# Windowed attention and two feed-forward layers in one kernel: output sums behind a group's last products, three PSUM tiles in the last group, conversions moved beside h, and another start address for x's operands

## The chip, the cores and the metric

The kernel runs on one core of a Trainium2 chip. The metric is the device time in microseconds; lower is better. Its engines are named as in the profile: PE multiplies matrices (PEld loads its stationary operand), DVE, ACT and POOL work element by element, and SP issues most of the DMAs. PE accumulates in PSUM, from which DVE and ACT read.

## What is computed

Windowed attention over q, k, v (4 batches, 8 heads, 576 positions, window 64) gives x of 2304 x 512. Two feed-forward layers follow; the change is in the second and in the end of the first:

```python
a, b = x @ w1, x @ w2
x2 = (a * b @ w3) @ w_out          # first layer, 2304 x 512
h = x2 @ w_in                      # second layer, 2304 x 2048
g = h * (1 / (1 + np.exp(-h)))
out = g @ w_out2                   # 2304 x 512
```

## The kernel before

Every float32 product is made of three passes over a high and a low part of each operand (`PASSES`). The program is written out by hand in one order for each engine, and an engine runs its instructions in that order; a scheduler moves nothing.

The part around the change has four stages.

- **Phase a, block 5** (`phase_a(NBLK - 1, hooks5)`): the last block of 384 tokens of the first layer, 16 steps of 12 matmuls (L693) and 96 more (L723). Four PSUM accumulators take turns. ACT copies every other one out (L707), DVE multiplies the next by the copy (L709), ACT and POOL split the product. `hooks5` puts the first operands of stage h between these steps: loads of x2 and w_in32, sums of them, splits (`x_sum`, `x_op`, `w_part`).
- **Stage h**: h by Strassen's scheme with 7 products for each d of 12 (3 supers of 768 tokens by 4 duos of features); a product is 12 matmuls 384 wide. `h_slot` issues one product, then its read-out (`read`: DVE sums, ACT silu), then what the table `jobs` holds for that slot. Four sums of silu(h) per d go to DRAM (`keep`, tensor `gd`). A **conversion** (`convert`) turns two blocks of w_out2 from 64-bit words into float32 with sums, and stores them in DRAM (`t32`): ten slots of loads, ACT scalings (L220, L225), DVE bit operations (L228, L884), POOL adds. Conversions 0 and 1 stand in block 5, 2 to 7 in stage h, by the table `PLAN`.
- **The passage** from h to the output: the jobs of the last super load the converted weights (`o_load`), split them (`o_part`), and prepare the first output operands from `gd` (`f_load`, `f_sums`, `f_high`, `f_low`). Output products 0 to 3 are issued between the last products of h.
- **Output**: 36 output products (`out_products(m)`), each 42 matmuls 256 wide; four of them (e = 0 to 3) make a group, 128 rows on either side. Product m needs `hi` and `lo` of m, in one of four sets that take turns, so that `f_high(m + 3)` waits until product m - 1 has read its set. A group accumulates in two PSUM tiles, `a` and `b`, of two banks each; odd and even groups use different ones. `out_sums` makes the output of a group's seven terms: an ACT copy of A11, four DVE adds and a last one, each called as soon as its term's last matmuls (e = 3) are issued:

```python
                if e == DUOS - 1:
                    out_sums(tg, op)
```

The terms S2 and S3 share bank 1 of `a`, S1 and A22 share bank 0 of `a`, A12 and S4 bank 0 of `b`. A tile is guarded as a whole: a matmul that is issued after a sum of the same tile waits for that sum. In the pool `end` a tile of 96 bytes, `e0`, stands ahead of the tiles x0 to x6 that hold x's operands (`xop`), so each starts 96 bytes past a multiple of 128; the operands of phase a (xa, xb, p, q) start at multiples of 128.

Of the kernel before, what the change touches and what calls it, by code (L numbers as in the profile page):

```python
# [9 lines left out]
F32 = mybir.dt.float32  # L10
# [32 lines left out]
def tile_window_attention_ffn(ctx, tc, qkv, qkp, vp, w1, w2, w3t, w_out, w_in, w_out2, out):  # L43
# [7 lines left out]
    nc = tc.nc  # L51
# [3 lines left out]
    dram = ctx.enter_context(tc.tile_pool(name="dram", bufs=1, space=DRAM))  # L55
# [76 lines left out]
    class Chunk:  # L132
# [14 lines left out]
        begun = False  # L147
# [600 lines left out]
    with tc.manual_schedule():  # L748
# [5 lines left out]
        for i in range(16):  # L754
            qq, k = divmod(i, 4)
# [34 lines left out]
        OPS = 7  # L790
        POS = (0, 1, 6, 2, 4, 3, 5)
        HALF = slice(0, NB), slice(NB, 2 * NB)
        gd = dram.tile([NTG, DUOS, 128, 4, 256], F32, name="gd", tag="gd")
        t32 = dram.tile([PAIRS, 128, 7, 256], F32, name="t32", tag="t32")
        xop, raw, wop, oop = {}, {}, {}, {}
        g, bank, tmp = {}, {}, {}
# [5 lines left out]
        def add(eng, out, a, b):  # L802
            tt(eng, out, a, b, ALU.add)
# [220 lines left out]
        def silu(out, src):  # L1024
            nc.scalar.activation(out=out, in_=src, func=AF.Silu)

        def keep(d, op, t):
            j, e = divmod(d, DUOS)
            nc.sync.dma_start(
                out=gd[3 * j : 3 * j + 3, e, :, op, :].rearrange("t p n -> p t n"),  # L1030
                in_=t.rearrange("p t q n -> p t (q n)"),
            )

        def read(d, k):

# [94 lines left out]


        A11, A12, A22, S1, S3, S2, S4 = range(7)
        TERMS = ((A11, 0, 0), (S2, 2, 1), (S3, 0, 1), (S1, 2, 0), (A22, 3, 0), (A12, 1, 0), (S4, 1, 1))
        AT = (("b", 1, 0), ("a", 1, 0), ("a", 1, 1), ("a", 0, 1), ("a", 0, 0), ("b", 0, 0), ("b", 0, 1))
        FIRST = (True, True, False, True, False, True, False)

        def out_products(m):
            tg, e = divmod(m, DUOS)
            if e == 0:
                for x, y in (("a", "ha"), ("b", "hb")) if tg % 2 == 0 else (("a", "hc"), ("b", "hd")):  # L1140
                    bank[x] = pso.tile([128, 2, 512], F32, name=f"o{x}{tg}", tag=y)
            lo, hi, a = sets.pop(m)
            for (op, w, half), (x, y, z), first in zip(TERMS, AT, FIRST):
                dst = bank[x][:, y, z * 256 : z * 256 + 256]
                for q in range(2):
                    cols = slice(q * 128, q * 128 + 128)
                    lhs = [x[:, cols] for x in a] if op == S4 else [hi[:, op, cols], lo[:, op, cols]]
                    rhs = [x[:, half] for x in oop[2 * e + q][w]]
                    for n, (l, r) in enumerate(PASSES):
                        nc.tensor.matmul(  # L1150
                            dst, lhsT=lhs[l], rhs=rhs[r], start=(first and e == 0 and q == 0 and n == 0),
                            stop=(e == DUOS - 1 and q == 1 and n == 2), skip_group_check=True,
                        )
                if e == DUOS - 1:
                    out_sums(tg, op)

        def out_sums(tg, op):

            a, b = bank["a"], bank["b"]
# [6 lines left out]
            row = j * 2 * NB + r * 128  # L1169
            if op == A11:  # L1170
                nc.scalar.copy(out=one, in_=b[:, 1, 0:256])
            elif op == S2:
                add(nc.vector, two, a[:, 1, 0:256], one)
            elif op == S3:
                add(nc.vector, u3, a[:, 1, 256:512], two)
            elif op == S1:
                add(nc.vector, u4, a[:, 0, 256:512], two)
            elif op == A22:
                x = a[:, 0].rearrange("p (i n) -> p i n", i=2)
                add(nc.vector, c[:, 1], x, t[:, 3:4].to_broadcast([128, 2, 256]))  # L1180
                nc.sync.dma_start(out=out[row + NB : row + NB + 128, :], in_=c[:, 1].rearrange("p i n -> p (i n)"))
            elif tg == NTG - 1:
                i = 1 if op == S4 else 0
                add(nc.vector, c[:, 0, i], b[:, 0, i * 256 : i * 256 + 256], t[:, i])
                (nc.sync if i else nc.scalar).dma_start(
                    out=out[row : row + 128, i * 256 : i * 256 + 256], in_=c[:, 0, i]
                )
            elif op == S4:
                add(nc.vector, c[:, 0], b[:, 0].rearrange("p (i n) -> p i n", i=2), t[:, 0:2])
                nc.sync.dma_start(out=out[row : row + 128, :], in_=c[:, 0].rearrange("p i n -> p (i n)"))  # L1190


        X5 = {2: (x_sum, 0), 3: (x_op, 0, 0), 4: (x_sum, 2), 5: (x_sum, 1), 7: (x_op, 0, 1), 9: (x_op, 0, 2)}
# [3 lines left out]
        def hooks5(n):  # L1197
            run_later()
            if n == 0:
                tmp["t1"] = xe[:, 1536:2304].rearrange("p (k n) -> p k n", k=2)  # L1200
                x_raw(0)
                e0 = end.tile([128, 24], F32, name="e0", tag="e0")[:, 0:1]
                nc.gpsimd.memset(e0, 0.0)
                silu(e0, e0)
                places = [slot(f"wd{i}", f"x{i}", [1024], pool=end) for i in range(2, 6)]
                for i, (first, x) in enumerate(((2, 2), (6, 0))):
                    convert(i, n5 + first, places[x : x + 2])
                r_load(0, slot("r0", "x6", [1024], pool=end))
# [22 lines left out]
        for j in range(1, SUPER):  # L1231
# [10 lines left out]
        for n, first in ((0, 2), (1, 10), (2, 12), (3, 16), (4, 18), (5, 23), (6, 24)):  # L1242
            for part in range(4):
# [3 lines left out]
        at(FIRST_OUT + 22, f_load, 0)  # L1247
        at(FIRST_OUT + 22, f_load, 1)
        at(FIRST_OUT + 24, f_sums, 0, nc.vector)
        at(FIRST_OUT + 25, f_high, 0)  # L1250
        at(FIRST_OUT + 26, f_low, 0)
        at(FIRST_OUT + 26, f_sums, 1, nc.vector)
        at(FIRST_OUT + 27, f_load, 2)
        at(FIRST_OUT + 27, o_load, 7)

        phase_a(NBLK - 1, hooks5)
# [126 lines left out]
```

## Time and profile before

| | |
|---|---|
| median of 3 runs | 892.2 us (889.32 to 894.3) |
| profiled execution | 890.85 us |
| its span (first to last instruction) | 888.3 us, mean granted clock 0.976 |
| PE busy | 831.2 us (94%) |
| DVE / ACT / POOL busy | 656.5 / 542.5 / 388.1 us |

Times in rows are microseconds from the span's start. The profiled execution lies 2.5 us over its own span and 1.35 us under the median. A busy PE is the time in which some matmul is under way; how fast they follow each other has to be read from their starts.

### The profile page before, as it was taken

To read this page: it belongs to the slowest core of one execution; us is meant where nothing else is said; L and a number is where in the kernel's file an instruction comes from. 1 tells how busy PE (TensorE), PEld (TensorE's weight loads), DVE (VectorE), ACT (ScalarE), POOL (GpSimd) and SP (SyncE) were. 2 spreads that over 40 slices of the span, in tenths; PEclk is the share of its full clock that TensorE was granted. 3 is DMA by queue.
4 is the path that set the end of the run, shared out by engine and by line. 5 is a ranking of instruction groups with operands and counts; after the bars stand their busy time and mean duration, and the time that the engine had idled before them with its cause. 6 is when DMAs were issued, how large, how long until landed. Compare 5 with 4: busy or idle time off the path is not lost. (4 is left out here: it accounts for less than half of the span.)

```text
span 888.3 us, 15643 instructions
## 1 busy us (share of the span) xinstructions
PE 831.2 (94%) x5066; PEld 779.0 (88%) x5066; DVE 656.5 (74%) x1527; ACT 542.5 (61%) x1290; POOL 388.1 (44%) x468
## 2 busy tenths in 40 slices
PE   8899999999999999999879999999984988888887
PEld 3455899999999999999779999999984988888887
DVE  8879777788888888882885798665688667677561
ACT  7889778898898998984554555444553333333230
POOL 5767666677776776774651243400002111111100
PEclk9999999999999999999999999999987899899899
DMA  9997235345445455435234879968755233233210
GB/s 309 337 293 237 76 99 165 108 138 186 135 149 173 138 163 168 148 99 179 112 131 131 247 232 278 303 189 243 240 187 160 95 119 119 96 120 112 89 61 24
DMA packets 78256, 146.34 MB, mean 165 GB/s; under 512 B 7136, under 2 KB 46432, under 8 KB 78176
## 3 DMA queue, kind: packets, MB, share of 16 engines
q1 hardware_dynamic: 74576, 140.50, 49.0%
q10 hardware_dynamic: 3600, 4.85, 1.5%
q8 instruction: 40, 0.66, 0.3%
q14 instruction: 40, 0.33, 0.1%
HBM read 105.48 MB, written 39.85 MB: 164 GB/s over the span
## 5 line engine op out<-in xcount | busy, mean ns | idle before, releaser
L693 PE MATMUL ab<-xa,hl 128*128 128x384 f32 x576 | 119.7, 342 | 5.0 <-DVE a L709 3.4
L1150 PE MATMUL oa<-wo_w,hi 128*128 128x256 f32 x432 | 85.5, 293 | 32.4 <-DVE ot L800 32.4
L693 PE MATMUL ab<-xb,hl 128*128 128x384 f32 x570 | 115.2, 334 | 0.0
L693 PEld LDWEIGHTS ab<-xa,hl 128*128 128x128 f32 x576 | 98.7, 188 | 6.8 <-DVE a L709 4.5
L1150 PEld LDWEIGHTS oa<-wo_w,hi 128*128 128x128 f32 x432 | 67.8, 194 | 38.4 <-DVE ot L800 38.4
L693 PEld LDWEIGHTS ab<-xb,hl 128*128 128x128 f32 x570 | 100.3, 188 | 0.0
L800 POOL TENSOR_TENSOR fs<-f 128x256 f32<-128x256 f32 x11 | 10.2, 928 | 153.0 <-DMA f<-gd 141.0
L351 POOL TENSOR_TENSOR klo<-qk,qkhi 64x192 fp32r<-64x192 f32 x110 | 67.3, 612 | 8.4 <-ACT qkhi L345 2.3
L723 PE MATMUL x<-p,wp 128*128 128x384 f32 x360 | 69.9, 342 | 0.0
L474 POOL TENSOR_TENSOR xr<-ot 128x128 f32<-128x128 f32 x55 | 32.7, 595 | 72.8 <-DVE ot L473 56.0
L723 PEld LDWEIGHTS x<-p,wp 128*128 128x128 f32 x360 | 62.8, 191 | 0.0
L1150 PE MATMUL oa<-wo_w,lo 128*128 128x256 f32 x216 | 61.9, 286 | 0.0
L406 ACT ACTIVATE sm<-sm,nm 128x192 f32<-128x192 f32 x110 | 49.3, 449 | 1.4
L1016 PE MATMUL hd<-xop,wi_w 128*128 128x384 f32 x252 | 48.5, 339 | 0.2 <-DVE gxb L800 0.2
L1016 PE MATMUL ha<-xop,wi_w 128*128 128x384 f32 x252 | 48.5, 339 | 0.1
L1016 PE MATMUL hb<-xop,wi_w 128*128 128x384 f32 x252 | 48.4, 339 | 0.0
L1119 ACT CAST hi<-gq 128x768 fp32r<-128x768 f32 x26 | 20.5, 832 | 44.3 <-issue 42.9
L345 ACT CAST qkhi<-qk 128x768 fp32r<-128x768 f32 x55 | 45.9, 835 | 1.2
L392 DVE CUSTOM_DVE_ANT_0 sm<-s,consts 128x192 f32<-128x192 f32 x144 | 45.2, 351 | 1.3 <-PE s L385 0.9
L1016 PEld LDWEIGHTS hd<-xop,wi_w 128*128 128x128 f32 x252 | 44.6, 188 | 0.6 <-DVE gxb L800 0.6
L1016 PEld LDWEIGHTS ha<-xop,wi_w 128*128 128x128 f32 x252 | 44.6, 188 | 0.5 <-ACT gxb L1041 0.4
L1016 PEld LDWEIGHTS hb<-xop,wi_w 128*128 128x128 f32 x252 | 44.7, 188 | 0.0
(257 smaller groups left out, 2353.1 us busy)
## 6 DMA issues: line engine op xcount, KB each, us to landing
qk<-in_qkv SPq DMA_DIRECT2D x55, 384.0 KB, 3.0
words<-in_w3t SPq DMA_DIRECT2D x16, 512.0 KB, 6.9
words<-in_w SPq DMA_DIRECT2D x16, 512.0 KB, 7.0
xe<-in_w_in SPq DMA_DIRECT2D x16, 512.0 KB, 4.7
gd<-gxa SPq DMA_DIRECT2D x18, 384.0 KB, 4.4
gd<-gst SPq DMA_DIRECT2D x18, 384.0 KB, 6.1
gq<-gd SPq DMA_DIRECT2D x13, 512.0 KB, 3.3
gq<-in_w_out SPq DMA_DIRECT2D x12, 512.0 KB, 5.2
```

The lines of the kernel that those rows point to most:

```text
L345: nc.scalar.copy(out=hi, in_=t)
L351: nc.gpsimd.tensor_tensor(out=k_lo[g % 2][hs, h * 192 : h * 192 + 192], in0=t[hs, n], in1=f32(hi[hs, n]), op=ALU.subtract)
L392: nc.vector.tensor_tensor_reduce(out=sm[g % 2][:, h, :], in0=s_ps[:, h, :], in1=consts[:, at + 64 - 64 * h : at + 256 - 64 * h], op0=ALU.a ...
L406: nc.scalar.activation(out=e[:, h, :], in_=x, func=AF.Exp, scale=-1.0, bias=nm[:, h : h + 1], accum_out=sums_of[g % 2][:, h, 0:1])
L474: nc.gpsimd.tensor_tensor(out=xr[:, c, r : r + 128], in0=t[:, 0:128], in1=t[:, 128:256], op=ALU.add)
L693: nc.tensor.matmul(acc, lhsT=w[:, l, fs], rhs=x[k // 2][:, k % 2, r, :], start=(k == 0 and n == 0), stop=(k == 3 and n == 2),)
L723: nc.tensor.matmul(acc, lhsT=wp[f][:, l, o * 128 : (o + 1) * 128], rhs=p[f][:, r, :], start=(f == 0 and n == 0), stop=(f == 7 and n == 2),)
L800: eng.tensor_tensor(out=out, in0=a, in1=b, op=op)
L1016: nc.tensor.matmul(bank[name][:, q, 0:NB], lhsT=w[:, l, first + kt], rhs=x[:, kt, r, :], start=(fresh and kt == 0 and n == 0), stop=(kt == ...
L1119: nc.scalar.copy(out=hi[:, i : i + 3], in_=x[:, 0:768].rearrange("p (a n) -> p a n", a=3))
L1150: nc.tensor.matmul(dst, lhsT=lhs[l], rhs=rhs[r], start=(first and e == 0 and q == 0 and n == 0), stop=(e == DUOS - 1 and q == 1 and n == 2 ...
```

## The change

The sums of a group are called only after all products of e = 3, except in the last group. There they stay between the terms, but the terms lie in three tiles, with S2 and S3 in one, S1 and A22 in another, A11, A12 and S4 in the third. Conversions 0 and 1 leave block 5: `PLAN` now has all eight in stage h, five slots apart, from slot 12. `e0` is allocated behind x's tiles, which moves these to multiples of 128 bytes. `gd` keeps the three groups of a super side by side, so a write has one run of 3 KB per partition where it had three of 1 KB, and a read four of 1 KB where it had one of 4 KB. In the passage, the loads of output products 0 and 1 go ahead of an `o_load`, `f_sums(1)` goes behind the last slot, and half of `o_part(6)` behind output product 0.

```diff
-        gd = dram.tile([NTG, DUOS, 128, 4, 256], F32, name="gd", tag="gd")
+        gd = dram.tile([SUPER, DUOS, 128, 4, 768], F32, name="gd", tag="gd")
...
+            nc.sync.dma_start(out=gd[j, e, :, op], in_=t.rearrange("p t q n -> p (t q n)"))
...
-            nc.sync.dma_start(out=t[0], in_=gd[tg, e].rearrange("p a n -> p (a n)"))
+            cols = slice(tg % 3 * 256, tg % 3 * 256 + 256)
+            nc.sync.dma_start(out=t[0].rearrange("p (a n) -> p a n", a=4), in_=gd[tg // 3, e, :, :, cols])
...
+        ORDER = (A11, S2, S3, S1, A22, A12, S4)
...
+        AT_END = {A11: ("a", 1, 0), S2: ("b", 0, 0), S3: ("b", 0, 1), S1: ("c", 0, 1), A22: ("c", 0, 0)}
+        AT_END |= {A12: ("a", 0, 0), S4: ("a", 0, 1)}
+        END_FIRST = (A11, S2, S3, A12, S4, S1, A22)
...
-                if e == DUOS - 1:
+                if e == DUOS - 1 and last:
                     out_sums(tg, op)
+            if e == DUOS - 1 and not last:
+                for op in ORDER:
+                    out_sums(tg, op)
...
-                e0 = end.tile([128, 24], F32, name="e0", tag="e0")[:, 0:1]
-                nc.gpsimd.memset(e0, 0.0)
-                silu(e0, e0)
-                places = [slot(f"wd{i}", f"x{i}", [1024], pool=end) for i in range(2, 6)]
-                for i, (first, x) in enumerate(((2, 2), (6, 0))):
-                    convert(i, n5 + first, places[x : x + 2])
...
+            if n == 20:
+                e0 = end.tile([128, 24], F32, name="e0", tag="e0")[:, 0:1]
...
-        PLAN = ((2, 12), (3, 18), (4, 25), (5, 31), (6, 37), (7, 43))
+        PLAN = tuple((n, 12 + 5 * n) for n in range(PAIRS))
...
+        for n, first in ((0, 2), (1, 10), (2, 12), (3, 16), (4, 18), (5, 23), (6, 26)):
+            for part in range(4 if n < 6 else 2):
...
+        for k, f, m in ((22, f_load, 0), (22, f_load, 1), (25, f_high, 0), (26, f_low, 0)):
+            jobs.setdefault(FIRST_OUT + k, []).insert(0, lambda f=f, m=m: f(m))
+        jobs.setdefault(FIRST_OUT + 24, []).insert(0, lambda: f_sums(0, nc.vector))
...
+        f_sums(1, nc.vector)
         f_high(1)
```

On PE, the last product of group 1 (m = 7) before, from its second term on; `oa1` and `ob1` are the group's two tiles. The waits stand in brackets:

```order
L1150 MATMUL oa1_8097<-wo_w19_7714,hi7_8087 128x256 [waits Activation_49]
L1150 MATMUL oa1_8097<-wo_w19_7714,hi7_8087 128x256
L1150 MATMUL oa1_8097<-wo_w19_7714,lo7_8086 128x256 [waits DVE_49]
L1150 MATMUL oa1_8097<-wo_p_7875,hi7_8087 128x256 x2
L1150 MATMUL oa1_8097<-wo_p_7875,lo7_8086 128x256
L1150 MATMUL oa1_8097<-wo_w17_7712,hi7_8087 128x256 [waits DVE_49]
...
L1150 MATMUL oa1_8097<-wo_w19_7714,hi7_8087 128x256 [waits DVE_49]
...
L1150 MATMUL oa1_8097<-wo_w20_7694,hi7_8087 128x256 [waits DVE_49]
...
L1150 MATMUL ob1_8098<-wo_w18_7713,hi7_8087 128x256 [waits Activation_49]
```

The same terms in the changed kernel:

```order
L1160 MATMUL oa1_8093<-wo_w19_7757,hi7_8083 128x256 [waits Activation_49]
L1160 MATMUL oa1_8093<-wo_w19_7757,hi7_8083 128x256
L1160 MATMUL oa1_8093<-wo_w19_7757,lo7_8082 128x256 [waits DVE_49]
L1160 MATMUL oa1_8093<-wo_p_7871,hi7_8083 128x256 x2
L1160 MATMUL oa1_8093<-wo_p_7871,lo7_8082 128x256
L1160 MATMUL oa1_8093<-wo_w17_7755,hi7_8083 128x256 x2
...
L1160 MATMUL oa1_8093<-wo_w19_7757,hi7_8083 128x256 x2
...
L1160 MATMUL oa1_8093<-wo_w20_7690,hi7_8083 128x256 x2
...
L1160 MATMUL ob1_8094<-wo_w18_7756,hi7_8083 128x256 x2
```

The matmuls stand in the same order; the waits at the head of the third, fourth, fifth and sixth term are gone, those for `hi` and `lo` stay.

On DVE in the passage, before: `gq` and `xe` rows of x4 are `f_sums` of output products 0 and 1, `lo` and `a` are `f_low`, `wo_w` is `o_part`, `gxb` and `hc` are the read-out of h:

```order
L800 TENSOR_TENSOR gst_6177<-hd_5_7619,gst_6177 128x768
L800 TENSOR_TENSOR wo_w_7691<-gst_6178,wo_w_7691 128x512
L800 TENSOR_TENSOR gq<-gq 128x256 x4
L800 TENSOR_TENSOR wo_w_7692<-gst_6178,wo_w_7692 128x512
L800 TENSOR_TENSOR wo_w_7712<-or_7671,wo_w_7712 128x512
L800 TENSOR_TENSOR gxb<-hb_1_7657,gxb 128x768
L800 TENSOR_TENSOR hc_4_7721<-hc_4_7721,gxb 128x3x2x128
L800 TENSOR_TENSOR wo_w_7693<-gst_6179,wo_w_7693 128x512
L800 TENSOR_TENSOR wo_w_7694<-gst_6179,wo_w_7694 128x256
L800 TENSOR_TENSOR wo_w_7713<-or_7671,wo_w_7713 128x512
L800 TENSOR_TENSOR lo_7739<-gq,hi_7740 128x768 x2
```

And in the changed kernel:

```order
L800 TENSOR_TENSOR gst_6121<-hd_5_7615,gst_6121 128x768
L800 TENSOR_TENSOR gq<-gq 128x256 x4
L800 TENSOR_TENSOR wo_w_7687<-gst_6122,wo_w_7687 128x512
L800 TENSOR_TENSOR wo_w_7688<-gst_6122,wo_w_7688 128x512
L800 TENSOR_TENSOR gxb<-hb_1_7653,gxb 128x768
L800 TENSOR_TENSOR hc_4_7712<-hc_4_7712,gxb 128x3x2x128
L800 TENSOR_TENSOR lo_7726<-gq,hi_7727 128x768 x2
L800 TENSOR_TENSOR a_7725<-gq,a_7725 128x256
L800 TENSOR_TENSOR wo_w_7689<-gst_6123,wo_w_7689 128x512
L800 TENSOR_TENSOR wo_w_7690<-gst_6123,wo_w_7690 128x256
```

`lo` of output product 0 has moved ahead of three weight splits, which follow later; nothing has left the row of work.

On ACT at the start of block 5, before: `cv_b` and `cv_r` are the scalings of conversion 0, `wd` its loaded words, `a` the copies out of PSUM that free an accumulator:

```order
L1025 ACTIVATE e_5653<-e_5653 128x1
L701 COPY a_0_5675<-ab_0_5663 128x384
L114 CAST p_5648<-a_0_5675 128x384
L220 ACTIVATE cv_b<-wd_5658 128x512
L225 ACTIVATE cv_r<-wd_5658 128x512
L707 COPY a_1_5713<-ab_2_5700 128x384
L971 CAST xop_0_5715<-xra_5650 128x2x384
```

In the changed kernel:

```order
L701 COPY a_0_5667<-ab_0_5655 128x384
L114 CAST p_5648<-a_0_5667 128x384
L707 COPY a_1_5700<-ab_2_5687 128x384
L971 CAST xop_0_5702<-xra_5650 128x2x384
```

The copy `a_1` no longer stands behind a scaling that waits for the load of `wd`.

## Rows read from the trace of the kernel before

**Rows 1.** Windows by stage: stretch, length, busy time (count) of PE, PEld, DVE, ACT, POOL.

```profile
410.50:471.80 61.30, 52.99 (x289) 50.97 (x289) 41.52 (x52) 27.85 (x52) 34.15 (x29) 0.97 0.43 150
497.00:537.00 40.00, 39.69 (x223) 38.81 (x222) 34.97 (x44) 24.30 (x37) 16.42 (x14) 1.00 0.86 262
649.40:685.80 36.40, 21.35 (x150) 20.96 (x151) 33.53 (x58) 16.16 (x27) 4.79 (x5) 0.81 0.53 167
685.80:886.00 200.20, 178.62 (x1374) 172.45 (x1374) 121.88 (x216) 56.65 (x95) 23.67 (x27) 0.94 0.26 93
```

**Rows 2.** Who waited for whom, PE, 685.9 to 886: total, times, longest.

```profile
PE oa L1150 <- DVE ot L800: 32.4, 27, 12.1
```

**Rows 3.** The chain that ended last, output stage: start, duration, what.

```profile
784.67 0.35 DVE ot L800
...
791.16 2.81 PE oa L1150 x24
793.98 2.12 PE ob L1150 x18
796.10 2.81 PE oa L1150 x24
...
807.71 0.35 DVE ot L800
...
885.23 0.42 DVE oc L800
```

**Rows 4.** Timeline of the passage, DVE and PE: start, duration, [idle before, releaser].

```profile
645.70 1.55 DVE L800 TENSOR_TENSOR gq<-gq 128x256 f32<-128x256 f32 x4 [2.18 <-DMA gq<-gd]
...
677.54 0.41 DVE L800 TENSOR_TENSOR a<-fs,a 128x256 fp32r<-128x256 f32 x1
...
685.34 0.41 DVE L800 TENSOR_TENSOR ot<-oa,ot 128x256 f32<-128x256 f32 x1
685.80 0.80 PE L1150 MATMUL oa<-wo_w,hi 128*128 128x256 f32 x2 [12.15 <-DVE ot L800]
```

**Rows 5.** Who waited for whom, PE, block 5 (410 to 473).

```profile
PE ab L693 <- DVE a L709: 3.4, 2, 2.0
PE x L723 <- ACT q L114: 3.3, 1, 3.3
PE ab L693 <- ACT a L707: 1.6, 1, 1.6
```

**Rows 6.** Timeline, ACT in block 5.

```profile
423.14 0.66 ACT L220 ACTIVATE cv_b<-wd 128x512 f32<-128x512 f32 x1 [7.12 <-DMA wd<-in_w_out]
455.98 0.62 ACT L856 CAST wi_w<-r 128x512 fp32r<-128x512 f32 x1 [2.56 <-DMA r<-w_in]
```

**Rows 7.** Groups by line, DVE, block 5: busy, mean ns, idle before.

```profile
L228 DVE TENSOR_SCALAR cv_b<-cv_b 128x512 int32<-128x512 int32 x4 | 4.4, 1108 | 8.4 <-DMA wd<-in_w_out 8.4
L884 DVE SCALAR_TENSOR_TENSOR cv_b<-wd,cv_b 128x512 int32<-128x512 int32 x4 | 3.4, 838 | 0.0
```

**Rows 8.** Timeline, PE: matmuls 384 wide, operands xa, xb, then xop.

```profile
416.74 1.20 PE L693 MATMUL ab<-xa,hl 128*128 128x384 f32 x6
...
420.90 1.20 PE L693 MATMUL ab<-xa,hl 128*128 128x384 f32 x6
...
638.13 2.28 PE L1016 MATMUL hd<-xop,wi_w 128*128 128x384 f32 x12
640.25 1.22 PE L1016 MATMUL ha<-xop,wi_w 128*128 128x384 f32 x6
```

**Rows 9.** Timeline, ACT, PE and DVE in stage h.

```profile
513.09 0.67 ACT L220 ACTIVATE cv_b<-gq 128x512 f32<-128x512 f32 x1 [1.94 <-DMA gq<-in_w_out]
...
540.61 2.28 PE L1016 MATMUL hb<-xop,wi_w 128*128 128x384 f32 x12
...
544.76 0.94 DVE L800 TENSOR_TENSOR gxb<-hb,gxb 128x768 f32<-128x768 f32 x1
```

**Rows 10.** DMA issues, page: count, KB each, us to landing.

```profile
gq<-in_w_out SPq DMA_DIRECT2D x12, 512.0 KB, 5.2
```

More of the change, by code (lines that the diff above doesn't have):

```diff
@@ L1028, in keep @@
             j, e = divmod(d, DUOS)
[L1029 to L1032, printed above, removed]
+            nc.sync.dma_start(out=gd[j, e, :, op], in_=t.rearrange("p t q n -> p (t q n)"))
         def read(d, k):
@@ L1132, in tile_window_attention_ffn @@
         A11, A12, A22, S1, S3, S2, S4 = range(7)
-        TERMS = ((A11, 0, 0), (S2, 2, 1), (S3, 0, 1), (S1, 2, 0), (A22, 3, 0), (A12, 1, 0), (S4, 1, 1))
-        AT = (("b", 1, 0), ("a", 1, 0), ("a", 1, 1), ("a", 0, 1), ("a", 0, 0), ("b", 0, 0), ("b", 0, 1))
-        FIRST = (True, True, False, True, False, True, False)
+        TERMS = {A11: (0, 0), S2: (2, 1), S3: (0, 1), S1: (2, 0), A22: (3, 0), A12: (1, 0), S4: (1, 1)}
+        ORDER = (A11, S2, S3, S1, A22, A12, S4)
+        AT = {A11: ("b", 1, 0), S2: ("a", 1, 0), S3: ("a", 1, 1), S1: ("a", 0, 1), A22: ("a", 0, 0)}
+        AT |= {A12: ("b", 0, 0), S4: ("b", 0, 1)}
+        AT_END = {A11: ("a", 1, 0), S2: ("b", 0, 0), S3: ("b", 0, 1), S1: ("c", 0, 1), A22: ("c", 0, 0)}
+        AT_END |= {A12: ("a", 0, 0), S4: ("a", 0, 1)}
+        END_FIRST = (A11, S2, S3, A12, S4, S1, A22)
         def out_products(m):
             tg, e = divmod(m, DUOS)
+            last = tg == NTG - 1
             if e == 0:
-                for x, y in (("a", "ha"), ("b", "hb")) if tg % 2 == 0 else (("a", "hc"), ("b", "hd")):
-                    bank[x] = pso.tile([128, 2, 512], F32, name=f"o{x}{tg}", tag=y)
+                for x, y in (("a", "ha"), ("b", "hb"), ("c", "hc")) if tg % 2 == 0 else (("a", "hc"), ("b", "hd")):
+                    if x != "c" or last:
+                        bank[x] = pso.tile([128, 2, 512], F32, name=f"o{x}{tg}", tag=y)
             lo, hi, a = sets.pop(m)
-            for (op, w, half), (x, y, z), first in zip(TERMS, AT, FIRST):
+            places = AT_END if last else AT
+            begun = set()
+            for op in END_FIRST if last and e == 0 else ORDER:
+                w, half = TERMS[op]
+                x, y, z = places[op]
                 dst = bank[x][:, y, z * 256 : z * 256 + 256]
+                first = (x, y) not in begun
+                begun.add((x, y))
                 for q in range(2):
@@ L1153, in out_products @@
                         )
-                if e == DUOS - 1:
+                if e == DUOS - 1 and last:
+                    out_sums(tg, op)
+            if e == DUOS - 1 and not last:
+                for op in ORDER:
                     out_sums(tg, op)
         def out_sums(tg, op):
-            a, b = bank["a"], bank["b"]
+            last = tg == NTG - 1
             if op == A11:
@@ L1169, in out_sums, with src, both @@
             row = j * 2 * NB + r * 128
+            def src(op):
+                x, y, z = (AT_END if last else AT)[op]
+                return bank[x][:, y, z * 256 : z * 256 + 256]
+            def both(op):
+                x, y, _ = (AT_END if last else AT)[op]
+                return bank[x][:, y].rearrange("p (i n) -> p i n", i=2)
             if op == A11:
-                nc.scalar.copy(out=one, in_=b[:, 1, 0:256])
-            elif op == S2:
-                add(nc.vector, two, a[:, 1, 0:256], one)
+                nc.scalar.copy(out=one, in_=src(A11))
@@ L1174, in out_sums @@
             elif op == S3:
-                add(nc.vector, u3, a[:, 1, 256:512], two)
-            elif op == S1:
-                add(nc.vector, u4, a[:, 0, 256:512], two)
+                add(nc.vector, two, src(S2), one)
+                add(nc.vector, u3, src(S3), two)
             elif op == A22:
-                x = a[:, 0].rearrange("p (i n) -> p i n", i=2)
-                add(nc.vector, c[:, 1], x, t[:, 3:4].to_broadcast([128, 2, 256]))
+                add(nc.vector, u4, src(S1), two)
@@ L1181, in out_sums @@
+                add(nc.vector, c[:, 1], both(A22), t[:, 3:4].to_broadcast([128, 2, 256]))
                 nc.sync.dma_start(out=out[row + NB : row + NB + 128, :], in_=c[:, 1].rearrange("p i n -> p (i n)"))
[L1182 to L1187, printed above, removed]
-            elif op == S4:
-                add(nc.vector, c[:, 0], b[:, 0].rearrange("p (i n) -> p i n", i=2), t[:, 0:2])
-                nc.sync.dma_start(out=out[row : row + 128, :], in_=c[:, 0].rearrange("p i n -> p (i n)"))
+            elif op == S4 and not last:
+                add(nc.vector, c[:, 0], both(A12), t[:, 0:2])
+                nc.sync.dma_start(out=out[row : row + 128, :], in_=c[:, 0].rearrange("p i n -> p (i n)"))
+            elif op == S4:
+                for i, x in ((0, A12), (1, S4)):
+                    add(nc.vector, c[:, 0, i], src(x), t[:, i])
+                    (nc.sync if i else nc.scalar).dma_start(
+                        out=out[row : row + 128, i * 256 : i * 256 + 256], in_=c[:, 0, i]
+                    )
@@ L1214, in hooks5 @@
                 r_load(3, xe)
+            if n == 20:
+                e0 = end.tile([128, 24], F32, name="e0", tag="e0")[:, 0:1]
+                nc.gpsimd.memset(e0, 0.0)
+                silu(e0, e0)
             if n == 22:
@@ L1239, in tile_window_attention_ffn @@
                 at(s + k, x_op, j, x)
-        PLAN = ((2, 12), (3, 18), (4, 25), (5, 31), (6, 37), (7, 43))
+        PLAN = tuple((n, 12 + 5 * n) for n in range(PAIRS))
         FIRST_OUT = 7 * DUOS * (SUPER - 1)
-        for n, first in ((0, 2), (1, 10), (2, 12), (3, 16), (4, 18), (5, 23), (6, 24)):
-            for part in range(4):
+        for n, first in ((0, 2), (1, 10), (2, 12), (3, 16), (4, 18), (5, 23), (6, 26)):
+            for part in range(4 if n < 6 else 2):
                 at(FIRST_OUT + first + part, o_part, n, part)
@@ L1246, in tile_window_attention_ffn @@
             at(FIRST_OUT + first, o_load, n)
[L1247 to L1253, printed above, removed]
+        for k, f, m in ((22, f_load, 0), (22, f_load, 1), (25, f_high, 0), (26, f_low, 0)):
+            jobs.setdefault(FIRST_OUT + k, []).insert(0, lambda f=f, m=m: f(m))
+        jobs.setdefault(FIRST_OUT + 24, []).insert(0, lambda: f_sums(0, nc.vector))
+        at(FIRST_OUT + 26, f_load, 2)
         at(FIRST_OUT + 27, o_load, 7)
@@ L1281, in tile_window_attention_ffn @@
         keep(NDUO - 1, 2, g["a22"])
+        o_part(6, 2)
+        o_part(6, 3)
         f_sums(2, nc.vector)
```

## The prediction

> **What bounds the kernel now.** I read the windows by stage first. In the output stage (685.8 to 886) PE is busy 178.6 of 200.2 us at a mean granted clock of 0.94, while DVE has 121.9 us of work and ACT 56.7: nobody is full [rows 1]. The list of who waits for whom says why: PE stood 32.4 us in 27 waits for DVE's output sums `ot`, once for 12.1 us [rows 2]. The chain that ended last gives the price for one group. From one `ot` on it (784.67) to the next (807.71) are 23.0 us. A product without a wait runs from 791.16 to 796.10, 4.94 us for its 24 + 18 matmuls, 0.1177 us each; four make 19.8 us [rows 3]. So a group loses 3.3 us. The reader is to see that `ot` runs for only 0.35 us: the wait is one of order. PE issues the next term while DVE is in another term's sum of the same tile.
>
> In the passage it is the other way round. From 649.4 to 685.8 DVE is busy 33.5 of 36.4 us (92%), PE 21.4, at a clock of 0.81 [rows 1]: here DVE's own work bounds. The timeline shows its end: `a` of product 4 is done at 677.95, the sums of group 0 come only at 685.34, after the operands of products 5 and 6, and PE has stood 12.15 us in the middle of product 3 [rows 4].
>
> Block 5 lasts 61.3 us [rows 1] for 16 x 12 + 96 = 288 matmuls. At the pace there (0.1733 us, below) that is 49.9, so 11.4 are lost: 8.3 in the three waits named [rows 5], and by the clock of 0.97 [rows 1] some 1.8 at the lower of the two levels (1.2 for 2.4 GHz). In the middle of stage h, 497 to 537, PE is busy 39.7 of 40 us and DVE 35.0 [rows 1]: PE bounds, with DVE close behind.
>
> **Block 5: conversions gone.** There ACT's first scaling waits 7.12 us for its words `wd` [rows 6], in front of the copy `a` that frees an accumulator (the order shows that). DVE waits for the same load 8.4 us in all, and has 4.4 + 3.4 = 7.8 us of bit operations for the two conversions [rows 7]. A later 2.56 us wait of ACT is for the load `r` of w_in [rows 6], whose queue held the conversions' stores as well. DVE has 41.5 busy of 61.3 us [rows 1], so nothing else there is full. The three waits (8.3) go, and the clock stays up: -10.5. Bounds: -11.4 if all that is lost comes back, -7 if the 2.56 us wait and a little more stay.
>
> **x's operands at multiples of 128.** Two rows show two paces for matmuls of the same width. With xa from 416.74 to 420.90, 24 matmuls take 4.16 us, 173.3 ns each; with xop from 638.13 to 640.25, 12 take 2.12 us, 176.7 ns [rows 8]. The operands differ in their start address, but also in their stationary partner and in what DVE and the DMAs do at the time. If the address makes the difference, 84 slots x 12 = 1008 matmuls x 3.4 ns are 3.5 us. No row separates the causes; I take -3.5, bounds -3.5 and 0. The pace holds in full since PE is full there.
>
> The Trainium skill, "TensorE: Matmul & The Clock Gate", "Back-to-back issue gap", gives the distance of two matmuls by their width alone, without a term for where the operand starts. By it the move is worth nothing and the sum is 3.5 us higher; this case's rows show two paces for one width, which speaks against it but does not name the cause.
>
> **Two more conversions beside h.** DVE's part of one is 7.8 / 2 = 3.9 us [rows 7]. One every five slots (5 x 2.12 = 10.6 us) instead of every 6.2 slots (13.1 us) adds 3.9 x 40 x (1/10.6 - 1/13.1) = 2.8 us in 40 to DVE's 35.0 [rows 1]: 37.8, 95%, without the adds of `cv_t`, which stand in another group. That fits, but a late read-out then has less room to catch up. ACT's wait for `gq` of w_in_out at a conversion's start is 1.94 us, and a read-out (`gxb<-hb`) at 544.76 starts 1.9 us after PE's last matmul into its accumulator (540.61 + 2.28) [rows 9]. I take +2 (a quarter of a us at each of eight), from 0 to +8 (1 us at each of eight). Memset and `silu` of e0, which move into the slots, are ACT and POOL work of well under 1 us beside PE's: 0; without cover the same fraction once.
>
> **Passage and output.** DVE keeps its work in the passage; weight splits change places with output operands (the second pair of orders), and half of `o_part(6)` goes behind. The first `gq` sums there waited 2.18 us for their load from `gd` [rows 4], which now goes ahead of an `o_load`. What it can start earlier is 0 to 2.2; I take 1.3. Operands of product 4 are then done at 677.95 - 1.3 = 676.7. Product 3, no longer stopped by sums, has 12 of its 42 matmuls out by 673.6 and needs 30 x 0.1177 = 3.5 more: 677.1. So product 4 starts at about 677 (675.5 to 680, the late end if PE pauses ahead of product 3 and the clock falls). Then 32 products x 4.94 [rows 3] without waits: 158.1, and PE ends at 835.1.
>
> Do the operands and sums hold this pace? DVE's 121.9 us of work lie on 1374 / 168 = 8.2 groups [rows 1], 14.9 us each. All sums stand behind product e = 3, so DVE waits for its end and for ACT's copy of A11; whatever is queued behind them, the operands of the next products, waits too. DVE reaches the sums at most 4.94 us before that end, 2.5 in the middle, plus about 0.4 for the copy: 14.9 + 2.9 = 17.8 of 19.8 us. The tiles of the next group are the other pair, so PE has 19.8 us until it needs this one again, and the sums end about 3 us behind the product. The 3.3 us a group, the 12.15 stop and most time at the low clock go. Before, the last sum on the chain starts at 885.23 [rows 3]; with one more 0.4 us sum behind the last product the tail is 0.4 longer. So the term is 885.2 - 835.1 = -50.1 (-44 to -51.6), tail +0.4.
>
> **`gd`'s layout.** A write has 3 KB runs, a read 1 KB runs. No row prices a read of such runs. In the output a read is issued a whole group (19.8 us) ahead, against 5.2 us to land for a 512 KB load [rows 10], so even three times that is hidden: 0. In the passage it is not a group ahead; there the 1.3 us above would go, within the range.
>
> **Sum.** 888.3 - 10.5 - 3.5 + 2 - 50.1 + 0.4 = 826.6. The profiled execution lies 2.5 us over its span: 829.1. It is 1.35 us under the median: 830.
>
> **Rivals.**
> 1. *The conversions hold stage h up.* DVE at 95% and `gxb` late already [rows 1, 9] speak for it; that a conversion's 3.9 us lie in pieces between read-outs speaks against it. +1 to +2.5 us at each of eight instead of +2 in all: 836 to 848, about 842.
> 2. *DVE becomes the bound behind the passage.* If it reaches the sums early each time, and ACT's `hi` come late behind its copies, a group takes 21 to 22 us in place of 19.8 (17.8 + 4 would do it): 8.2 x 1.2 to 2.2 is +10 to +18, about 845.
> 3. *The address is worth nothing,* all else as forecast: 833.5. The two paces [rows 8] would come from the stationary partner or the traffic.
> 4. *The sums still stop PE,* since a wait stays that the order does not show as one; then the output gains only the passage and the 2 us around it: about 878. The order has these waits gone.
> 5. *Slower.* A conversion is a chain: load, ACT, DVE, POOL, store, and the next one's words need the same two places. If one chain lasts longer than its five slots, each delays the read-outs behind it on DVE. The gains above are 62 us, so it decides at 62 / 8 = 7.8 us more for each, at a chain of 10.6 + 7.8 = 18.4 us: then 892 and more. A load of 5.2 us [rows 10] and operations of 0.6 to 1.1 us [rows 6, 7] speak against it.
>
> **Chances.** Forecast 0.63 (its own range 823 to 838, from the bounds of the terms), rival 1 0.17, rival 2 0.08, rival 3 0.08, rival 4 0.02, rival 5 0.02. Range 823 to 850: rivals 1 to 3 lie mostly inside it, so it leaves out no more than 2 in 10. A measurement of this kernel tells a change of about 0.5% (4.5 us) from none. Faster by more: all but rival 5 and a remainder, 0.96; within 0.02; slower 0.02.
>
> **What the profile after would show.** In the output PE's waits for `ot` are gone but for the last group, a group's period is 19.8 us, the granted clock is 1.00 from about 685 on. In stage h matmuls start 173 to 174 ns apart and the stage begins about 461; matmuls 176.7 ns apart there would refute the address. In block 5 no wait of PE is over about 1 us. PE's idle time in stage h at slots 12 to 52 is under 2 us in all; above 8 it is rival 1. PE pauses ahead of output product 3 and not within it. The prediction is wrong if the sums' wait returns as one for `hi` or `lo` (a period over 21 us), or if stage h grows.

## The result, and the profile after

The changed kernel takes 830.3 us (median of 4 runs, 828.78 to 831.39) against 891.7 us for the kernel before beside it: a ratio of 0.931, 95% interval 0.928 to 0.934. Ratios are estimated from all runs of both kernels, so they can differ by a few thousandths from the quotient of the medians. The profiled execution spans 829.6 us, 58.7 us less than before. The forecast was 830 us, with 823 to 850 as its range.

The windows by stage of the changed kernel (columns as in [rows 1], then granted clock, DMA share, GB/s):

```profile
411.80:461.70 49.90, 49.90 (x289) 49.90 (x289) 30.41 (x40) 23.82 (x44) 23.84 (x21) 1.00 0.33 106
461.70:637.00 175.30, 173.68 (x998) 172.49 (x997) 127.72 (x175) 94.98 (x148) 49.22 (x44) 1.00 0.75 262
486.90:526.90 40.00, 38.38 (x218) 37.38 (x217) 37.40 (x49) 25.13 (x39) 19.69 (x17) 1.00 0.80 278
637.00:664.60 27.60, 24.67 (x183) 23.97 (x182) 25.92 (x47) 16.12 (x27) 2.71 (x3) 0.94 0.52 172
664.60:826.00 161.40, 161.40 (x1346) 161.23 (x1344) 130.91 (x228) 58.81 (x98) 28.03 (x29) 1.00 0.40 121
```

The reader is to see two stages in which PE never stops: block 5 (49.90 of 49.90 us, 61.3 before) and the output (161.40 of 161.40 us at a clock of 1.00, where [rows 1] has 178.6 of 200.2 at 0.94). The list of who waits for whom, PE from 640 to 830, has only the passage left in it; the 32.4 us of [rows 2] are gone:

```profile
PE ob L1160 <- DVE lo L800: 1.7, 1, 1.7
PE oa L1160 <- DVE lo L800: 0.4, 1, 0.4
```

The timeline of the changed kernel, DVE and PE (two products of stage h, the first `f_sums` of the passage, output product 3, and the first matmuls of products 4, 8 and 12):

```profile
463.80 2.24 PE L1016 MATMUL hb<-xop,wi_w 128*128 128x384 f32 x12
465.88 2.24 PE L1016 MATMUL ha<-xop,wi_w 128*128 128x384 f32 x12
...
632.72 1.55 DVE L800 TENSOR_TENSOR gq<-gq 128x256 f32<-128x256 f32 x4 [2.84 <-DMA gq<-gd]
...
655.44 0.40 PE L1160 MATMUL ob<-wo_w,hi 128*128 128x256 f32 x2
657.51 0.39 PE L1160 MATMUL ob<-wo_w,lo 128*128 128x256 f32 x1 [1.67 <-DVE lo L800]
...
658.92 0.38 PE L1160 MATMUL oa<-wo_w,lo 128*128 128x256 f32 x1 [0.43 <-DVE lo L800]
...
659.50 0.62 PE L1160 MATMUL oa<-wo_w,hi 128*128 128x256 f32 x2
...
664.60 0.41 PE L1160 MATMUL ob<-o0b,hi 128*128 128x256 f32 x2
...
684.76 0.40 PE L1160 MATMUL ob<-o0b,hi 128*128 128x256 f32 x2
...
704.92 0.40 PE L1160 MATMUL ob<-o0b,hi 128*128 128x256 f32 x2
```

In stage h a product of 12 matmuls takes 465.88 - 463.80 = 2.08 us, 173.3 ns each, where [rows 8] has 2.12. In the output a group takes 704.92 - 684.76 = 20.16 us: no stop, and yet 0.4 us more than the 4 x 4.94 = 19.76 worked out from [rows 3]. A product takes 5.04 us in place of 4.94, a matmul 120.0 ns where [rows 3] gives 117.6 (117.9 on average over the whole output stage before). This was not forecast, and the first three experiments go to it.

The chain that ended last closes in the changed kernel with PE, at 824.60 + 1.45 = 826.05; 3.6 us of sums and of the last store follow, where 3.1 followed before [rows 3]:

```profile
824.60 1.45 PE oa L1160 x12
```

### The profile page after: what moved, and what is told of

Read it like the earlier page. It is cut to its first block, busy times and chain, and to the rows that moved or that the text cites. A ratio compares the mean times of both kernels' runs of the same rounds, so it can differ in the third digit from the quotient of the medians.

```text
span 829.6 us, 15630 instructions
## 1 busy us (share of the span) xinstructions
PE 811.6 (98%) x5066; PEld 766.6 (92%) x5066; DVE 653.8 (79%) x1527; ACT 543.7 (66%) x1290; POOL 389.8 (47%) x468
## 4 chain that ended last, share of the span: by engine, by line
PE 66%; DVE 7%; ACT 7%; POOL 6%; issue 5%; DMA 1%; ACTq 0%; SPq 0%; DVEq 0%; POOLq 0%
PE ab L693 15%; PE oa L1160 11%; PE x L723 8%; PE ob L1160 8%; PE ha L1016 4%; PE hb L1016 4%; PE hd L1016 4%; PE hc L1016 2%; PE accw L614 2%; POOL klo L351 2%; PE t L428 2%; POOL vhl L369 1%; POOL p L117 1%; PE o L462 1%; POOL xr L474 1%
## 5 line engine op out<-in xcount | busy, mean ns | idle before, releaser
L1160 PE MATMUL oa<-wo_w,hi 128*128 128x256 f32 x408 | 77.9, 285 | 0.0
L1160 PEld LDWEIGHTS oa<-wo_w,hi 128*128 128x128 f32 x408 | 63.6, 191 | 0.0
L1160 PE MATMUL oa<-wo_w,lo 128*128 128x256 f32 x204 | 58.3, 286 | 0.4 <-DVE lo L800 0.4
L428 PE MATMUL t<-consts,sm 128*128 128x128 f32 x216 | 35.9, 275 | 7.4 <-DVE sm L418 5.3
```

The source lines that it names most:

```text
L428: nc.tensor.transpose(t_ps[:, i * 128 : i * 128 + 128], x[:, at : at + 128], id_sb)
L1160: nc.tensor.matmul(dst, lhsT=lhs[l], rhs=rhs[r], start=(first and e == 0 and q == 0 and n == 0), stop=(e == DUOS - 1 and q == 1 and n == 2 ...
```

## The experiments

**The operands' start address.** Three kernels differ from the changed one only in where x's seven tiles start. They hold xop in stage h (there the moving operand) and in the output hi and three of every four lo (there the stationary operands); the fourth lo lies in `xa`, which stays at a multiple of 128. For 96 bytes:

```diff
             if n == 0:
...
+                tmp["e0"] = end.tile([128, 24], F32, name="e0", tag="e0")[:, 0:1]
...
             if n == 20:
-                e0 = end.tile([128, 24], F32, name="e0", tag="e0")[:, 0:1]
+                e0 = tmp["e0"]
```

> The changed kernel, but x's tiles start 96 bytes past a multiple of 128 again; nothing else moves. Theory 1 (the start address of the operands sets both paces): stage h goes back from 173.4 to about 176.7 ns per matmul, +3.3 us over its 1008 matmuls, and the output, whose stationary operands hi and lo lie in the same tiles, goes back from 120.0 to about 117.7 ns, -3.3 us over its 32 products; the two cancel and the time stays within 1.5 us of the changed kernel (830.3). Rival A (the address only acts in stage h; the slower output pace comes from running without stops): 176.7 in h, 120.0 in the output, time +3.3 us. Rival B (the address does nothing, the paces come with the other moves): 173.4 and 120.0, no change.

For 64 bytes; for 32 the two numbers change places:

```diff
+                end.tile([128, 16], F32, name="pad", tag="pad")
...
-                e0 = end.tile([128, 24], F32, name="e0", tag="e0")[:, 0:1]
+                e0 = end.tile([128, 8], F32, name="e0", tag="e0")[:, 0:1]
```

> The changed kernel with x's tiles 64 bytes past a multiple of 128. If the address acts by halves or quarters of 128 bytes: either as at 0 (173.4 ns in h, 120.0 in the output) or as at 96 (176.7, 117.7). If the moving operand of h and the stationary operand of the output want different things, one of the offsets could have 173.4 and 117.7 together, 3.3 us less than the changed kernel: about 827. Rival (the address does nothing): 173.4, 120.0, no change.

> The changed kernel with x's tiles 32 bytes past a multiple of 128. Same reading as for 64: theory 1 expects the two paces to change with the offset, about 176 ns in h and 117.7 in the output if 32 is as 96, and then the time of the changed kernel within 1.5 us; the rival without an effect of the address expects 173.4, 120.0 and no change.

Measured: 829.1, 828.1 and 829.3 us, ratios 0.926 [0.924, 0.929], 0.925 [0.923, 0.927] and 0.927 [0.924, 0.929]. The times lie too close together to tell much; the timelines do. One product of h and the first matmuls of output products 7, 8 and 12, offset 96:

```profile
462.09 2.28 PE L1016 MATMUL hb<-xop,wi_w 128*128 128x384 f32 x12
464.21 2.28 PE L1016 MATMUL ha<-xop,wi_w 128*128 128x384 f32 x12
...
679.54 0.40 PE L1160 MATMUL ob<-wo_w,hi 128*128 128x256 f32 x2
...
684.53 0.40 PE L1160 MATMUL ob<-o0b,hi 128*128 128x256 f32 x2
...
704.34 0.40 PE L1160 MATMUL ob<-o0b,hi 128*128 128x256 f32 x2
```

And offset 64, products 8 and 12:

```profile
462.94 2.24 PE L1016 MATMUL hb<-xop,wi_w 128*128 128x384 f32 x12
465.02 2.24 PE L1016 MATMUL ha<-xop,wi_w 128*128 128x384 f32 x12
...
684.15 0.40 PE L1160 MATMUL ob<-o0b,hi 128*128 128x256 f32 x2
...
703.99 0.40 PE L1160 MATMUL ob<-o0b,hi 128*128 128x256 f32 x2
```

From the starts of all matmuls that follow one another without a stop, on average:

| offset | ns in stage h | ns in the output | one output group |
|---|---|---|---|
| 0 (changed kernel) | 173.4 | 120.0 | 20.16 us |
| 32 | 175.5 | 118.4 | 19.88 us |
| 64 | 173.3 | 118.1 | 19.84 us |
| 96 | 176.7 | 117.9 | 19.81 us |

Theory 1 holds: both paces go with the address. An offset of 0 is, with 64, the best of the four in h, and it is the worst in the output. What h gains by it (1008 x 3.3 ns = 3.3 us) the output gives back (32 x 42 x about 2.1 ns = 2.8 us). Rivals A and B are out. At 64 both are near their best. How the two stationary operands act together is not shown: at 96 product 7, whose lo stays at a multiple of 128, takes 684.53 - 679.54 = 4.99 us, and the other three of a group (19.81 - 4.99) / 3 = 4.94; at 64, with that lo in the same place, all four take 4.96.

The mean for 32 hides something. Its timeline, across one stop:

```profile
518.11 2.24 PE L1016 MATMUL ha<-xop,wi_w 128*128 128x384 f32 x12
520.19 2.24 PE L1016 MATMUL hb<-xop,wi_w 128*128 128x384 f32 x12
...
525.23 2.38 PE L1016 MATMUL ha<-xop,wi_w 128*128 128x384 f32 x12 [0.72 <-ACT gxb L1038]
527.46 2.28 PE L1016 MATMUL hc<-xop,wi_w 128*128 128x384 f32 x12
529.58 2.28 PE L1016 MATMUL hb<-xop,wi_w 128*128 128x384 f32 x12
```

Up to the stop that ends at 525.23 a product takes 2.08 us; from 527.46 on it takes 2.12, and so to the end of the stage, with the same tiles at the same addresses. So at this offset both paces occur, and which one runs changed at a stop. With 0, 64 and 96 one pace ran through the stage in each profile.

**The output sums alone,** on the kernel before: `TERMS` to `out_sums` of the changed kernel, all else as before.

```diff
-                if e == DUOS - 1:
+                if e == DUOS - 1 and last:
                     out_sums(tg, op)
+            if e == DUOS - 1 and not last:
+                for op in ORDER:
+                    out_sums(tg, op)
```

> The kernel before with the new output sums alone (behind a group's last products, three tiles in the last group). My account: PE's waits for the sums go, group period 19.8 us at 117.7 ns, product 4 starts about 678, PE ends about 837, time 891.7 - 48 = 843 to 845. Rival (the sums alone shift the wait to hi and lo, because the passage still has its old order): a period over 21 us or a new stop behind the passage, time above 855.

Measured: 843.6 us, ratio 0.942 [0.940, 0.945]; the account gave 843 to 845 from 891.7, a ratio of 0.945 to 0.948, so the gain is a little larger than it said. Its window by stage and PE's longest wait from 640 on:

```profile
684.00:838.40 154.40, 154.36 (x1310) 154.16 (x1308) 126.64 (x223) 56.44 (x94) 26.77 (x28) 1.00 0.36 123
```

```profile
PE ob L1162 <- DVE lo L800: 2.8, 1, 2.8
```

PE is busy 154.36 of 154.40 us. The sums alone bring nearly all of the output's gain, and with the passage in its old order; the wait does not move to `hi` or `lo` behind it. The three tiles of the last group are part of this run, and no run separates them from the new place of the calls.

**The conversions alone,** on the kernel before:

```diff
-                places = [slot(f"wd{i}", f"x{i}", [1024], pool=end) for i in range(2, 6)]
-                for i, (first, x) in enumerate(((2, 2), (6, 0))):
-                    convert(i, n5 + first, places[x : x + 2])
...
-        PLAN = ((2, 12), (3, 18), (4, 25), (5, 31), (6, 37), (7, 43))
+        PLAN = tuple((n, 12 + 5 * n) for n in range(PAIRS))
```

> The kernel before with the eight conversions alone moved beside stage h (the new table, none in block 5). My account: block 5 falls from 61.3 to between 50 and 51 us, stage h loses 0 to 2 us more, the rest as before: 9 to 11 us faster, a ratio of about 0.989. Rival (DVE in stage h cannot take two more): stage h longer by 5 us or more, a ratio over 0.993.

Measured: 883.4 us against 892.6, ratio 0.986 [0.980, 0.992]. The windows of block 5 and stage h:

```profile
410.40:460.30 49.90, 49.90 (x289) 49.90 (x289) 29.23 (x40) 24.00 (x44) 23.05 (x21) 1.00 0.33 106
460.30:639.00 178.70, 177.06 (x998) 175.57 (x996) 126.84 (x176) 96.15 (x151) 49.33 (x44) 1.00 0.84 257
```

Block 5 gives back all of its 11.4 us. Stage h, from its first matmul to the output's first, lasts 178.7 us where it lasted 177.7: the price of the two conversions in it is 1.1 us in this pair of profiles. The interval of the ratio holds the account's 0.989 and ends just short of the rival's 0.993; the windows decide for the account.

**The address alone,** on the kernel before:

```diff
-                e0 = end.tile([128, 24], F32, name="e0", tag="e0")[:, 0:1]
-                nc.gpsimd.memset(e0, 0.0)
-                silu(e0, e0)
...
+            if n == 20:
+                e0 = end.tile([128, 24], F32, name="e0", tag="e0")[:, 0:1]
+                nc.gpsimd.memset(e0, 0.0)
+                silu(e0, e0)
```

> The kernel before with x's operands alone moved to multiples of 128. Stage h from 176.7 to 173.4 ns, -3.3 us. The output's matmuls from 117.7 to 120.0 ns; where PE waits for sums the group's period is set by DVE and PE taking turns, so the slower products add 0 to 3.3 us. Time between -3.3 and 0 against the kernel before, a ratio of 0.996 to 1.0. Rival (the slower output pace needs the new order of the sums): 117.7 there, the full -3.3 us.

Measured: 891.3 us against 892.6, ratio 0.997 [0.994, 0.999]. A product of h takes 2.08 us, but stage h, to the output's first matmul, is only 1.3 us shorter than before (176.4 in place of 177.7). PE now waits in it, 0.7, 0.6 and 0.2 us, where the list of the kernel before has one wait of 0.2. In the output PE waits for the sums as long as before. A product of h, the wait for the sums, and the waits in stage h:

```profile
475.32 2.24 PE L1016 MATMUL hb<-xop,wi_w 128*128 128x384 f32 x12
477.40 2.24 PE L1016 MATMUL ha<-xop,wi_w 128*128 128x384 f32 x12
```

```profile
PE oa L1150 <- DVE ot L800: 32.6, 27, 12.8
```

```profile
PE hb L1016 <- DVE wi_p L800: 0.7, 1, 0.7
PE ha L1016 <- ACT gxb L1041: 0.6, 1, 0.6
PE hd L1016 <- DVE gxb L800: 0.2, 1, 0.2
```

The output's matmuls run at 119.9 ns here too, so the slower pace does not need the new order of the sums. From the output's first matmul to PE's end it takes 234.5 us (235.7 before): while PE stops for sums, its pace costs nothing that can be seen.

**The passage in its old order,** on the changed kernel, profiled in two separate runs:

```diff
-        for n, first in ((0, 2), (1, 10), (2, 12), (3, 16), (4, 18), (5, 23), (6, 26)):
-            for part in range(4 if n < 6 else 2):
+        for n, first in ((0, 2), (1, 10), (2, 12), (3, 16), (4, 18), (5, 23), (6, 24)):
+            for part in range(4):
...
-        for k, f, m in ((22, f_load, 0), (22, f_load, 1), (25, f_high, 0), (26, f_low, 0)):
-            jobs.setdefault(FIRST_OUT + k, []).insert(0, lambda f=f, m=m: f(m))
-        jobs.setdefault(FIRST_OUT + 24, []).insert(0, lambda: f_sums(0, nc.vector))
-        at(FIRST_OUT + 26, f_load, 2)
+        at(FIRST_OUT + 22, f_load, 0)
+        at(FIRST_OUT + 22, f_load, 1)
+        at(FIRST_OUT + 24, f_sums, 0, nc.vector)
+        at(FIRST_OUT + 25, f_high, 0)
+        at(FIRST_OUT + 26, f_low, 0)
+        at(FIRST_OUT + 26, f_sums, 1, nc.vector)
+        at(FIRST_OUT + 27, f_load, 2)
...
-        f_sums(1, nc.vector)
...
-        o_part(6, 2)
-        o_part(6, 3)
```

> The changed kernel with the passage in its old order (loads, f_sums and o_part where they stood before); all else as changed. My term for the new order was 1.3 us, bounds 0 to 2.2: 1 to 2 us slower than the changed kernel, about 0.933 of the kernel before, with a stop of about 3 us within output product 0 as the kernel before has it. Rival (the order there is worth nothing, DVE's sum of work alone counts): the time of the changed kernel within 0.5 us.

> The kernel of the seventh run (the changed one with the passage in its old order) once more, now on one chip with the changed kernel: by the two traces product 5 of the output starts 1.0 us later after the start of stage h plus what stage h itself lost; so 0.5 to 2.5 us slower than the changed kernel. Rival (nothing): within 0.5 us.

The changed kernel ran beside the second of them, with this expectation:

> The changed kernel unaltered, beside the others on the same chip: 829 to 832, as in its first runs; its stages as in its first profile within 0.5 us each.

Measured: 831.5 us (ratio 0.929 [0.925, 0.933]) the first time; the second time 831.7 us (0.931 [0.928, 0.934]), beside the changed kernel's 830.6 (0.929 [0.925, 0.932]). The intervals overlap. In the traces I took the time from a matmul late in stage h (the 841st of 1008) to the first of output product 5, which leaves out what happened in h: 59.6 and 60.7 us with the old order, 59.6 and 60.1 with the new one. The stop of about 3 us within product 0 is back with the old order (2.83 us behind `lo`), but the one in product 3 is gone instead. Pair by pair the new order is worth -0.4 to 1.1 us (0.7 for the two that ran beside each other); neither expectation is decided.

In stage h rival 1 shows itself at one place, in both profiles with the old order. The timeline of the second, ACT and PE:

```profile
567.01 0.66 ACT L220 ACTIVATE cv_b<-gq 128x512 f32<-128x512 f32 x1 [3.35 <-DMA gq<-in_w_out]
...
571.13 1.15 PE L1016 MATMUL ha<-xop,wi_w 128*128 128x384 f32 x5 [2.12 <-ACT gxb L1038]
```

ACT's scaling waits 3.35 us for its words, and the read-out `gxb` behind it holds PE up for 2.12. In the first profile with the old order the same scaling waits 2.94 us and PE 0.84; in the two of the changed kernel it waits 0.86 and 1.44, and PE does not stop there. The edits of this kernel lie far behind this place, so why the load lands later is not shown. The stops lie ahead of the 841st matmul: they are in the 1.1 us between the medians, but not in the times from that matmul on.

**`gd` laid out as before,** on the changed kernel:

```diff
-        gd = dram.tile([SUPER, DUOS, 128, 4, 768], F32, name="gd", tag="gd")
+        gd = dram.tile([NTG, DUOS, 128, 4, 256], F32, name="gd", tag="gd")
...
-            cols = slice(tg % 3 * 256, tg % 3 * 256 + 256)
-            nc.sync.dma_start(out=t[0].rearrange("p (a n) -> p a n", a=4), in_=gd[tg // 3, e, :, :, cols])
+            nc.sync.dma_start(out=t[0], in_=gd[tg, e].rearrange("p a n -> p (a n)"))
```

> The changed kernel with gd laid out as before (writes in three runs of 1 KB, reads in one of 4 KB). My term was 0, since the reads in the output are issued a group ahead: the time of the changed kernel within 1 us, the group's period 20.16 us, and the first sums of the passage wait for their load about as long as in the changed kernel (2.84 us), within 1 us. Rival (reads in 1 KB runs cost time in the passage): that wait 1 us shorter or more, and product 4 of the output starts as much earlier.

Measured: 832.4 us, ratio 0.931 [0.928, 0.934], beside 830.6 and 0.929 on the same chip. The DMA issues in the page of the profile (KB each, us to landing), first of the changed kernel, then of this one:

```profile
gd<-gxa SPq DMA_DIRECT2D x18, 384.0 KB, 3.3
gd<-gst SPq DMA_DIRECT2D x18, 384.0 KB, 5.1
gq<-gd SPq DMA_DIRECT2D x13, 512.0 KB, 4.0
```

```profile
gd<-gxa SPq DMA_DIRECT2D x18, 384.0 KB, 4.8
gd<-gst SPq DMA_DIRECT2D x18, 384.0 KB, 5.8
gq<-gd SPq DMA_DIRECT2D x13, 512.0 KB, 3.4
```

The new layout makes a read 0.6 us slower and a write 0.7 to 1.5 us faster. From the 841st matmul of h to output product 5 it takes 59.5 us, as with the new layout. The first `gq` sums wait 3.55 us for their load, against 2.84 and 3.26 in the two profiles of the changed kernel: the rival is out, and in the passage the term is 0. The 1.8 us in the medians are more than the 1 us expected and are not settled: PE stops for 0.87 us in stage h of this profile, behind the scaling that the paragraph above shows (it waits 2.97 us here). That would be part of it, but one profile can't tie it to the layout.

**Offset 64, and `f_sums(3)` ahead of the last weight splits:**

```diff
+        f_sums(3, nc.vector)
         for part in range(4):
             o_part(7, part)
-        f_sums(3, nc.vector)
```

> The changed kernel with x's tiles at 64 past a multiple of 128 and with f_sums of output product 3 ahead of the last weight splits on DVE, which waits 1.42 us for ACT there. If the pause in product 3 (1.95 + 0.7 us, and 1.5 us at the lower clock) is set by DVE's queue, lo of product 3 comes 1.4 us earlier and the time falls by 1.4 to 3 us against the kernel with 64 alone, about 0.922 to 0.924 of the kernel before. Rival (the weights of the last splits are needed as early as lo): no change against it.

The timeline at offset 64 alone, DVE and PE:

```profile
652.63 2.23 DVE L800 TENSOR_TENSOR wo_p<-gst,wo_p 128x512 fp32r<-128x512 f32 x4 [1.42 <-ACT wo_p L962]
...
657.25 0.38 PE L1160 MATMUL ob<-wo_w,lo 128*128 128x256 f32 x1 [1.97 <-DVE lo L800]
```

Measured: 825.4 us (825.11 to 825.78), ratio 0.922 [0.918, 0.926], the fastest kernel here. Its timeline, DVE and PE:

```profile
650.03 1.54 DVE L800 TENSOR_TENSOR xe<-xe 128x256 f32<-128x256 f32 x4
651.54 2.24 DVE L800 TENSOR_TENSOR wo_p<-gst,wo_p 128x512 fp32r<-128x512 f32 x4
653.69 1.82 DVE L800 TENSOR_TENSOR lo<-xe,hi 128x768 fp32r<-128x768 f32 x2
...
654.70 0.39 PE L1160 MATMUL ob<-wo_w,lo 128*128 128x256 f32 x1 [0.53 <-DVE lo L800]
```

The sums now fill DVE's 1.42 us of waiting; PE's first wait in product 3 falls from 1.97 to 0.53 us and the second there, 0.44, is gone; one of 0.93 us for `lo` in product 4 is new. From the 841st matmul of h to product 5 it takes 57.45 us, against 60.14 with offset 64 alone: 2.7 us, as expected. The medians differ by as much, though the intervals of the two ratios overlap.

## Why the prediction was right

By its own steps, on the profiled executions (888.3 to 829.6 us, -58.7):

- **Block 5: right.** -10.5 was said, -11.4 came: all that was lost comes back, the upper bound. The experiment with the conversions alone shows the same 49.9 us.
- **x's operands: right in stage h, a term missing in the output.** 176.7 to 173.4 ns is -3.3 us (-3.5 said), and the three offsets show that the address does it; rival 3 and its 833.5 are out. The pace does not come through in full: with the address alone stage h is 1.3 us shorter, since PE then waits in it. What I did not see is that the tiles of x hold `hi` and `lo` later, so that the move reaches the output too. There it costs about 3 us.
- **Two more conversions in h: less than said, and in the changed kernel not to be told from nothing.** +2 was said; it is 1.1 us with the conversions alone. In the changed kernel stage h is 2.3 us shorter where the pace alone would give 3.3, and PE waits 1.6 us in it (0.7, 0.5 and 0.4). But with the address alone, without the conversions, it waits about as long, so this 1.0 us can't be put down to them. DVE is busy 37.4 of 40 us from 486.9 to 526.9 (37.8 was worked out), and PE loses 1.6 us of these 40. Rival 1 did not come; the late loads in the two profiles with the passage's old order and the one with the old `gd` (the longest 3.35 us, with a stop of 2.12) show how it would look.
- **Passage and output: the mechanism right, the size off by the pace.** -50.1 was said. From the output's first matmul to PE's end it is 235.7 us before, 189.0 after: -46.7. With offset 96, where the pace is that of before, it is 185.4: -50.3. So the mis-sized step is "32 products x 4.94": they take 5.04 each, 161.4 us with no stop in place of 158.1. The sums' waits are gone with the sums alone, as the account said; rivals 2 and 4 are out. DVE has 130.9 us of work in these 8 groups, 16.4 each of 20.16, where I worked out 14.9 of 19.8: it had less room than I thought, but enough (in the first of these groups it is busy 19.95 us of 20.16). Two stated bounds do not follow from their terms: product 4 at 680 gives -47.1 and not -44, and with every term at its best the sum is 822.2 for the span, so about 826 for the median and not 823. The measured -46.7 lies just outside -47.1 and inside -44.
- **The new order of the passage: not confirmed.** 1.3 us were said; -0.4 to 1.1 can be seen. The first sums do start earlier, 22.7 and 23.1 us behind the 841st matmul of h against 23.7 and 24.2 with the old order (they wait longer for their load, 2.84 and 3.26 us against 1.72 and 2.17, since they stand earlier in DVE's order). Little of that reaches product 5, because PE stops in product 3 instead of product 0. PE pauses inside product 3 at its first `lo`, not ahead of it as the prediction had it, and runs at a granted clock of 0.50, the lower level, from 659.5 to 662.7. Product 4 still starts where the account puts it: 677 less the 12.4 us by which the output begins earlier is 664.6, and it starts at 664.60. That is in part luck: what sets it is the end of product 3, late by its pauses and the clock, and `lo` of product 4, which the account had as the earlier bound, ends only 0.3 us before it.
- **The tail:** +0.4 said, +0.5 measured. **`gd`:** 0 said, 0 seen in the passage; 1.8 us between whole-kernel medians stay open.

The terms add up: block 5 -11.4, stage h -2.3, passage and output -46.7, tail +0.5, and +1.3 because block 5 itself begins at 411.8 in place of 410.5 in this execution (410.1 to 411.2 in the other profiles of kernels with this start). That is 3 us more than the 826.6 forecast for the span. The median still met the forecast, in part by luck: the profiled execution of before lay 2.5 us over its span and 1.35 under the median, and both were carried over, while the changed kernel's lies 1.8 us over its span and 1.1 over the median. These two make up the 3 us.

Rival 5, the slower one, did not come, though its condition was met. From its first load to the issue of its last store a conversion takes 16.8 to 23.8 us in the changed kernel, six of the eight more than 18.4. But the next one begins meanwhile: the last stores go out at 506.88 for the first and 581.36 for the eighth, 10.6 us apart on average, about the five slots of the table. So the length of one conversion was the wrong measure: long as they were, they did not hold one another up.

## What to carry to other kernels

When a consumer on another engine guards the accumulator that the producer still writes, calling it behind the last write, with the next group in other tiles as it already was, took out a wait here that cost 3.3 us a group, without any work removed. When a tile is moved, list every operand that ever lies in it, and in which role: the same start address was the best for the one role and the worst for the other. Before an order is rewritten, look for the engine's idle time just ahead of the late operand; one call moved into 1.42 us of waiting brought 2.7 us.

## What the runs showed of the hardware

The distance of two matmuls of one shape depended on where their operands start: 173.3 or 176.7 ns at 384 columns by the moving operand's offset from a multiple of 128 bytes, 117.9 to 120.0 ns at 256 columns by the stationary operand's. At an offset of 32 both paces of stage h occurred with the same addresses, 2.08 us for 12 matmuls up to a stop (two starts 1.06 us apart) and 2.12 from there on, so the address alone does not fix the pace. What does was not tried.
